# Moving sums, weight loads and a PSUM bank inside a fused attention and SiLU kernel

## The chip, the cores and the metric

The kernel runs on one core of one Trainium2 chip. The metric is the device time in microseconds (us). Three runs of the kernel before took 1318.69, 1319.69 and 1317.53 us, with a median of 1318.69.

## What is computed

The reference takes q, k and v of shape (8, 12, 448, 64), that is 8 batches of 12 heads with 448 positions. It divides each row of q and k by its root mean square and multiplies by a gain, forms softmax(q k^T / 8) v in each head, lays the heads side by side as x with 3584 rows and 768 columns, and computes a feed-forward block on it:

```
q_n, k_n = rmsnorm(q, g_q), rmsnorm(k, g_k)
attn = softmax(q_n @ k_n.T / sqrt(64))
x = (attn @ v).transpose(0, 2, 1, 3).reshape(3584, 768)
h = x @ w_in                       # 768 x 2048
out = (h * sigmoid(h)) @ w_out     # 2048 x 768
```

All inputs and the output are float32 numbers for the reference; w_in and w_out reach the chip as 64-bit words and are rounded to float32 by the kernel itself.

## The kernel before, in words

**Couples.** The attention works on 24 couples of head pairs (four heads each), three couples to a batch. In the code a couple is `c`, GROUP is 6 (the couples of two batches) and LATE is 12. For each couple, `visit(c)` issues the scores (L721), the exponentials on ScalarE (L726), and the weighted sums of v (`weigh`, L758) of this couple and the end of the last one. Then `between(c)` turns the next couple's q and k (`transpose_q` L638, `transpose_k` L656, both products with an identity on TensorE), sums the exponentials with products against ones (`sum_up`, L794), inverts the sums (L803, two halves), spreads the inverses over the partitions by DMA (`spread`, L810 and L812), and divides x by them (`divide`, L819).

**Seven products instead of eight.** The feed-forward block is computed in groups of two batches by a Strassen-type scheme (`Seven`): seven products of half-size blocks, whose operands are sums and differences. `sum_x` makes those of x: for each of three column blocks four VectorE operations of 128x448 (`right_sums`, L880, through `plus` and `minus`, L868 and L865). `sum_w_in` makes those of w_in, four steps of 128x768 for each of four chunks. A product takes six matmuls of 128x448 (L918). The products are evicted by ScalarE copies (L926, L936), VectorE sums (`plus`, L868) and GpSimd sums (L938, L939). Results of the first layer go through SiLU (L1056) and are stored to DRAM by `save` (L951).

**PSUM.** The pool ps_mm has two banks for products ("mm"). The pool ps has two tiles of two banks named "sc" (scores, transposes and, from couple 5 on, the sums of `sum_up`) and one bank each for "av0" and "av1". `bank(n)` hands out a product bank. In `sum_up` couples 0 to 4 take a product bank and couple 5 takes an "sc" tile.

**Order.** The order on every engine is that of the program text (the schedule is manual). `fill` deals the work of the products out between the couples: at every between-phase it advances a generator by a share of steps (one step is 448 columns, two matmuls), and deals a list of other pieces evenly over these steps, so that piece k of n falls after step total x k / n; a second list, `prompt`, gets one piece every three steps. From couple 6 to 11 the share is 13 steps a half. Products 1 and 2 of the first two blocks of the first group are made ahead, from couple 3 on (`make_ahead`), and kept in DRAM.

**Rounding of w_in.** `Rounder` brings 24 pieces of w_in (128x512 words of 64 bits, 0.5 MB each) in by SyncE DMAs (`load`, L85), splits them on ScalarE (`open`, L100 and L101), and rounds them on VectorE (L123, L126, L130) and GpSimd (L134) in `round`. Every `round` tries two more loads, each of which is issued when its buffer is free. The strings in `halves` and `visits` (L1388, L1389) say in which half of which couple pieces are opened ("o") and rounded ("r"). The sums of w_in are placed by `sums_halves` and `sums_visits`; those of the last chunk stand in couple 10:

```
sums_halves[8] = [(3, step) for step in range(4)]
```

**The first group's sums.** In `visit(6)`, after `divide(5)`, twelve VectorE operations make the sums of x for the first group, first steps 0 and 1 of the three column blocks, then steps 2 and 3. In `between(5)` the order is: sums of the exponentials, `divide(4)`, the two reciprocals and their DMAs, then the transposes for couple 6.

**The opening.** Before couple 0, TensorE runs unused products of the identity with itself (`keep_busy`, L407), six and then four. `transpose_q(0)` then turns q in two halves, each of which waits for VectorE's scaling of its rows (L511).

Of the kernel before, what the change touches and what calls it, by code (L numbers as in the profile page):

```python
# [11 lines left out]
F32 = mybir.dt.float32  # L12
# [15 lines left out]
BANK = 512  # L28
# [36 lines left out]
class Rounder:  # L65
# [3 lines left out]
    def __init__(self, nc, pieces):  # L69
        self.nc = nc  # L70
        self.pieces = pieces
        self.loaded = self.opened = self.rounded = 0

    def load(self):

# [29 lines left out]
    def round(self):  # L105

        i = self.rounded
        if i == len(self.pieces):
            return
        while self.opened <= i:
            self.open()
        self.rounded += 1
        dst, src, (_, raw), low = self.pieces[i]
        if src.dtype == I64:
            nc = self.nc  # L120
            wi = dst.bitcast(I32)
            high = raw.rearrange("p (n two) -> p n two", two=2)[:, :, 1]
            nc.vector.tensor_scalar(  # L123
                out=dst, in0=dst, scalar1=HIGH_MIN, scalar2=HIGH_MAX, op0=ALU.max, op1=ALU.min
            )
            nc.vector.tensor_scalar(  # L126
                out=wi, in0=wi, scalar1=3, scalar2=0x3FFFFFF8,
                op0=ALU.logical_shift_left, op1=ALU.bitwise_and,
            )
            nc.vector.scalar_tensor_tensor(  # L130
                out=wi, in0=high, scalar=-(1 << 30), in1=wi,
                op0=ALU.bitwise_and, op1=ALU.bitwise_or,
            )
            nc.gpsimd.tensor_tensor(out=wi, in0=wi, in1=low, op=ALU.add)  # L134
        for _ in range(2):
            self.load()


class Room:
# [6 lines left out]
    def __init__(self, nc, pool, w_in, z):  # L146
        P = z.P
        self.NC = z.NF // self.CHUNK
        self.size1 = z.NW * self.COLS
        self.size2 = 3 * z.NW // 2 * self.COLS // 2  # L150
        self.all = pool.tile([P, self.NC * (self.size1 + self.size2)], F32, name="W")
        self.rest = self.all[:, ds(self.NC * self.size1, self.NC * self.size2)]


        n = 2 * self.COLS
        bits = self.rest.bitcast(I32)
        pieces, before = [], {}
        for i in range(self.NC):
            for c in range(z.NW):
                number = len(pieces)  # L160
                raw = (number, number, 6 + number % 3, 7 + number % 2)[i]
                if 9 <= number < 12:
                    raw -= 6
                words = bits[:, ds(raw * n, n)]
                pieces.append(
                    (
                        self.chunk(i)[:, ts(c, self.COLS)],
                        w_in[ts(c, P), ts(i, self.COLS)],
                        (
                            before.get(raw),  # L170
                            words,
                        ),
                        words.rearrange("p (n two) -> p n two", two=2)[:, :, 0],
                    )
                )
                before[raw] = number
        self.w_in = Rounder(nc, pieces)

    def chunk(self, i):
        return self.all[:, ds(i * self.size1, self.size1)]  # L180
# [355 lines left out]
def bounded(  # L536
# [4 lines left out]
    HW, HF = z.NW // 2, z.NF // 2  # L541
# [87 lines left out]
    def transpose_q(c):  # L629

        t = ps.tile([P, 2, BANK], F32, name="sc", bufs=2)
        both = [t[:, i] for i in range(2)]
        if c == 0:
            both[1] = ps.tile([P, BANK], F32, name="av1")
        for i in range(2):
            for j in range(J):
                rows = q_of(c)[0:R, ts(i * J + j, 2 * D)]
                nc.tensor.transpose(both[i][:, ts(j, R)], rows, ident[0:R, 0:R])  # L638
            if c == 0:
                (nc.scalar.copy, nc.vector.tensor_copy)[i](qT[:, i], both[i][:, 0:S])  # L640
        if c > 0:
            nc.scalar.copy(qT, t[:, :, 0:S])
        if GROUP - 2 <= c <= GROUP:
            load_q(c + 2)
        elif c > GROUP + 1:
            load_q(c + 1)
# [129 lines left out]
    def sum_up(c):  # L776

        n = D // 2
        early = c < GROUP
        t = bank(S) if c < GROUP - 1 else ps.tile([P, 2, BANK], F32, name="sc", bufs=2)[:, 0, 0:S]
        terms = [(0, lambda: weights(c, 0))]
        if early:
            terms = [(0, lambda: weights(c, LEFT - 1))] + terms + [(1, None)]
        if c == GROUP - 1:
            terms.insert(1, (0, lambda: weights(c, 1)))
        for k, (which, w) in enumerate(terms):
            if k == len(terms) - 2:  # L790
                yield
            for h in range(2):
                for i in range(2):
                    nc.tensor.matmul(  # L794
                        t[ds(h * D + i * n, n), :],
                        ones[:, which + i if which else 0],
                        left_weights(c)[:, h] if which else w()[:, i, h],
                        start=(k == 0), stop=(k == len(terms) - 1),
                    )

        def invert(half):
            rows = ts(half, S // 2)
            nc.vector.reciprocal(out=factors(c)[0][:, rows], in_=t[:, rows])  # L803

        def spread():
            mine = [a.rearrange("(h i p) s -> i h p s", h=2, i=2) for a in factors(c)]
            queues = (nc.sync, nc.gpsimd if c == GROUP - 1 else nc.sync)
            for h in range(2):
                for i in range(2):
                    queues[h].dma_start(mine[1][i, h], mine[0][1, h])  # L810
            for h in range(2):
                queues[h].dma_start(mine[0][1, h], mine[0][0, h])  # L812

        yield [lambda: invert(0), lambda: (invert(1), spread())]
# [575 lines left out]
    for c in range(GROUP // 2):  # L1390
        halves[2 * (c - GROUP)], halves[2 * (c - GROUP) + 1] = "rr", "o"
    sums_halves = {-6: [(0, 0)], -4: [(0, 1)], -3: [(0, 2)], -2: [(0, 3)]}
    sums_halves[8] = [(3, step) for step in range(4)]
    sums_visits = {GROUP + 1: 1, GROUP + 3: 2}

    def weights_in(c, half):
# [14 lines left out]
    def visit(c):  # L1411
# [17 lines left out]
        if c > 0:  # L1429
            weigh(c - 1, LEFT - 1, 1)  # L1430
            if c - 1 < EARLY:
                for i in range(2):
                    nc.vector.tensor_copy(x_of(c - 1, i), sums[i])
                run_all(beside[1:2])
                if c == GROUP // 2 + 1:
                    divide(c - 2, None)
                if inverting:
                    while len(inverting) > 1:
                        inverting.pop(0)()
                    if c > 1:  # L1440
                        divide(c - 2, None)
            else:
                divide(c - 1, sums)
                if c == GROUP:
                    for steps in (range(2), range(2, 4)):
                        for i in range(HW):
                            sum_x(last_two(c), i, steps)
                run_all(beside[1:2])
                if GROUP < c < NC and c % GROUP == 0:
                    for i in range(1, HW):  # L1450
                        sum_x(last_two(c), i)
                weights_in_visit(c)
            if c + 1 < NC:
                loads["vrest"](c + 1)
# [28 lines left out]
    def run_all(work):  # L1483
        for piece in work:
            piece()

    def between(c):

        def transposes_and_sums():
            summing = sum_up(c)  # L1490
            if c < GROUP:
                next(summing)
            if c == GROUP - 1:
                reciprocals = next(summing)
                divide(c - 1, None)
                run_all(reciprocals)
                return
            if c < LATE - 1:
                transpose_k(c + 1)
            reciprocals = next(summing)  # L1500
            if LATE - 1 <= c < NC - 1:
                reciprocals += [lambda: flip(c + 1, "k"), gain]
            if GROUP // 2 < c < EARLY:
                divide(c - 1, None)
            return reciprocals
# [25 lines left out]
        if c >= LATE - 2:  # L1531
            if c == LATE - 2:
                prompt.append(pair_up)
            queries = prompt[3:] + [lambda: sum_squares(c + 2)]
            fill(weights_in(c, 1), prompt[:3] + [lambda: run_all(queries)])
        else:
            fill(weights_in(c, 1) + (further[:2] if c >= GROUP else []), prompt)
        if c % GROUP == GROUP - 1:
# [15 lines left out]
    load_q(2)  # L1554
    for _ in range(2):
        room.w_in.load()
    transpose_k(0)
    transpose_q(0)
    for c in range(NC):
# [230 lines left out]
```

## Time and profile before

| what | value |
|---|---|
| median of three runs | 1318.69 us |
| the profiled execution, device time | 1321.97 us |
| its span | 1320.2 us |
| TensorE matmuls busy (PE) | 1298.7 us, 98% |
| VectorE busy (DVE) | 951.1 us, 72% |
| ScalarE busy (ACT) | 505.4 us, 38% |
| GpSimd busy (POOL) | 362.6 us, 27% |
| mean granted TensorE clock | 0.995 |
| HBM traffic | 93.98 MB read, 41.29 MB written |

The profile is one execution on the chip. PE is TensorE's matmuls, PEld its weight loads, SP the engine that issues most DMAs. "L918" is line 918 of the kernel. In a timeline line the first number is the start in us, the second the duration, "x12" how many instructions are merged in the line, and the square brackets give the idle time of the engine before it and what ended that. The attention and the first layer take about the first 735 us of the span; after that TensorE runs the rest of the first layer and the second layer with hardly a pause.

### The profile page before, as it was taken

The page shows a single profiled execution, that of the slowest core. Times are in us where ns is not written, and L with a number is a line of the kernel's source. Part 1 is how long each engine was busy: PE and PEld are TensorE (multiplying, and loading weights), DVE is VectorE, ACT ScalarE, POOL GpSimd, SP SyncE. Part 2 cuts the span into 40 slices and gives each one's busy share as a digit, 9 for nine tenths or more (in the row PEclk, how much of TensorE's full clock was granted, in tenths as well). Part 3 has the DMA queues.
Part 4 walks back from the last instruction along what each step waited for, and adds up shares of the span by engine and source line. Part 5 has one row for each costly group of instructions (what it writes and reads, how often), then busy time and mean ns, then how long its engine had stood idle before and what let it go on. Part 6 is the DMA issues. An engine that isn't in the chain of part 4 may idle for free.

```text
span 1320.2 us, 19851 instructions
## 1 busy us (share of the span) xinstructions
PE 1298.7 (98%) x7201; PEld 833.0 (63%) x7201; DVE 951.1 (72%) x1627; ACT 505.4 (38%) x886; POOL 362.6 (27%) x230
## 2 busy tenths in 40 slices
PE   8999899999999999999999999999999999999998
PEld 4444444444444444444444455558999999999997
DVE  6998776785855555855554686698978787878785
ACT  7866555654555555454544244410000000000000
POOL 5765533353334333333420244410000000000000
PEclk9999899999999999999999999999999999999999
DMA  9675336333444444444321367412323233231411
GB/s 235 158 193 137 91 91 195 89 90 86 97 103 108 99 93 118 98 93 117 84 65 66 110 202 257 142 61 76 101 77 106 79 101 97 81 121 57 133 43 39
DMA packets 249439, 144.94 MB, mean 110 GB/s; under 512 B 184292, under 2 KB 233220, under 8 KB 249332
## 3 DMA queue, kind: packets, MB, share of 16 engines
q1 hardware_dynamic: 248672, 142.42, 38.7%
q8 instruction: 59, 0.97, 0.3%
q0 software_dynamic: 352, 0.96, 0.2%
q14 instruction: 48, 0.39, 0.1%
q10 hardware_dynamic: 308, 0.20, 0.1%
HBM read 93.98 MB, written 41.29 MB: 102 GB/s over the span
## 4 chain that ended last, share of the span: by engine, by line
PE 90%; DVE 3%; ACT 3%; issue 1%; DMA 1%; POOL 1%; SPq 0%; ACTq 0%; DVEq 0%; POOLq 0%
PE alone L1225 23%; PE mm L918 20%; PE sc L918 9%; PE av L758 9%; PE sc L721 8%; PE mm L1225 8%; PE alone L918 7%; PE alone L1262 2%; PE sc L794 1%; PE mm L794 1%; PE mm L1262 1%; ACT work L726 1%; DMA hidden<-stage 1%; PE sc L656 1%; DVE sums_x L865 1%
## 5 line engine op out<-in xcount | busy, mean ns | idle before, releaser
L726 ACT ACTIVATE work<-sc,rms 128x448 f32<-128x448 f32 x318 | 181.4, 634 | 66.2 <-PE sc L721 51.2
L918 PE MATMUL mm<-x,W 128*128 128x448 f32 x414 | 172.3, 552 | 6.3 <-DVE parts L868 4.1
L721 PE MATMUL sc<-work 64*64 64x448 f32 x1344 | 166.1, 548 | 1.7 <-ACT work L726 1.4
L772 DVE TENSOR_TENSOR work<-work 128x896 f32<-128x896 f32 (+1 forms) x114 | 124.5, 1125 | 51.4 <-PE av L758 50.9
L918 PE MATMUL mm<-sums_x,W 128*128 128x448 f32 x372 | 152.4, 543 | 1.9 <-DVE parts L868 1.9
L758 PE MATMUL av<-work,rows 64*64 64x448 f32 x1272 | 151.5, 540 | 0.7 <-DVE av L734 0.3
L496 POOL TENSOR_TENSOR rms<-rms,minus_half 128x14 f32<-128x14 f32 (+4 forms) x43 | 105.5, 2456 | 153.5 <-DVE rms L492 144.2
L918 PEld LDWEIGHTS mm<-x,W 128*128 128x128 f32 x414 | 77.8, 193 | 90.7 <-issue 75.6
L523 POOL DMA_DIRECT2D out_dram<-x x2 | 1.2, 592 | 443.3 <-DVE x L868 443.3
L918 PEld LDWEIGHTS mm<-sums_x,W 128*128 128x128 f32 x372 | 69.3, 190 | 74.8 <-issue 68.2
L1225 PE MATMUL alone<-W,rows 128*128 128x192 f32 x610 | 113.0, 326 | 0.0
L758 PEld LDWEIGHTS av<-work,rows 64*64 64x64 f32 x1272 | 57.0, 132 | 70.8 <-issue 33.9
L1225 PEld LDWEIGHTS alone<-W,rows 128*128 128x128 f32 x610 | 101.5, 190 | 0.0
L721 PEld LDWEIGHTS sc<-work 64*64 64x64 f32 x1344 | 53.5, 133 | 74.8 <-ACT work L726 30.9
L938 POOL TENSOR_TENSOR parts<-parts,stage 128x448 f32<-128x448 f32 x31 | 42.0, 1356 | 147.5 <-DVE parts L868 147.1
L918 PE MATMUL sc<-x,W 128*128 128x448 f32 x198 | 80.6, 543 | 0.0
L697 POOL TENSOR_TENSOR rms<-rms,minus_half 128x28 f32<-128x28 f32 x12 | 57.5, 4794 | 61.5 <-DVE rms L694 54.9
L1225 PE MATMUL alone<-W,work 128*128 128x192 f32 x382 | 72.2, 326 | 0.0
L1056 ACT ACTIVATE stage<-stage 128x896 f32<-128x896 f32 x63 | 57.4, 945 | 22.0 <-DVE stage L868 21.3
L803 DVE RECIPROCAL work<-sc 128x224 f32<-128x224 f32 x38 | 58.6, 1547 | 8.8 <-PE sc L794 8.6
L1235 ACT COPY rows<-alone 128x192 f32<-128x192 f32 x33 | 10.5, 318 | 141.5 <-PE alone L1225 78.1
L1225 PEld LDWEIGHTS alone<-W,work 128*128 128x128 f32 x382 | 63.8, 190 | 0.0
(258 smaller groups left out, 2262.8 us busy)
## 6 DMA issues: line engine op xcount, KB each, us to landing
hidden<-stage SPq DMA_DIRECT2D x63, 448.0 KB, 3.4
work<-hidden SPq DMA_DIRECT2D x21, 1024.0 KB, 5.2
rows<-in_moe_w_out_dram SPq DMA_DIRECT2D x32, 384.0 KB, 3.4
W<-in_moe_w_in_dram SPq DMA_DIRECT2D x22, 512.0 KB, 5.1
x<-hidden SPq DMA_DIRECT2D x7, 1024.0 KB, 5.6
work<-work SPq DMA_DIRECT2D x111, 56.0 KB, 2.0
rows<-in_q_dram SPq DMA_DIRECT2D x96, 56.0 KB, 2.2
rows<-in_k_dram SPq DMA_DIRECT2D x96, 56.0 KB, 2.2
```

Source lines behind the costliest of these rows:

```text
L496: nc.gpsimd.tensor_tensor(out=t, in0=t, in1=half, op=ALU.pow)
L697: nc.gpsimd.tensor_tensor(out=f, in0=f, in1=minus_half.to_broadcast([P, n]), op=ALU.pow)
L721: nc.tensor.matmul(two[ds(half * D, D), h, 0:S], keys[rows, ts(half, D)], qT[rows, pair, :], start=True, stop=True,)
L726: nc.scalar.activation(left_weights(c)[:, h] if j == LEFT else weights(c, j)[:, i, h], two[:, h, 0:S], AF.Exp, scale=norm.column(c, i, h, j),)
L758: nc.tensor.matmul(sums[i][ds(h * D, D), :], v, w, start=(j == 0 and step == 1), stop=(j == LEFT - 1 and step == 1),)
L772: nc.vector.tensor_tensor(out=total, in0=total, in1=more, op=ALU.add)
L803: nc.vector.reciprocal(out=factors(c)[0][:, rows], in_=t[:, rows])
L918: nc.tensor.matmul(t, self.left(name, s), self.right(name, s), start=s == ends[0], stop=s == ends[1])
L938: nc.gpsimd.tensor_tensor(out=u2, in0=u2, in1=p5, op=ALU.add)
L1056: nc.scalar.activation(t, t, AF.Silu)
L1225: nc.tensor.matmul(t, x[:, i], y, start=i == ORDER[0], stop=i == ORDER[-1])
L1262: nc.tensor.matmul(o, a[:, 2 * i + m, t], right_one(name, i)[:, m], start=n == 0, stop=n == len(steps) - 1,)
```

## The change

It has five parts. Four unused products are added in `transpose_q(0)`, two ahead of each half, into the bank "av0". The sums of couple 5 go into a product bank. The four operations of the first column block of `sum_x` for the first group move from `visit(6)` to `between(5)`, between `divide(4)` and the reciprocals. From piece 17 on, `Rounder` issues a load only if fewer than two pieces (three from piece 20 on) are loaded ahead of the rounding. The fourth step of the last chunk's w_in sums moves to the second half of couple 10, where the list of pieces is doubled with empty ones, so that it is dealt at the middle of the half.

```diff
@@ Rounder.__init__
         self.loaded = self.opened = self.rounded = 0
+        self.tight = len(pieces)
@@ Rounder.round
         for _ in range(2):
-            self.load()
+            if i < self.tight or self.loaded - self.rounded < 2 + (i > self.tight + 2):
+                self.load()
@@ Room.__init__
         self.w_in = Rounder(nc, pieces)
+        self.w_in.tight = 3 * z.NW - 1
@@ transpose_q
         for i in range(2):
+            if c == 0:
+                keep_busy(2)
             for j in range(J):
@@ sum_up
-        t = bank(S) if c < GROUP - 1 else ps.tile([P, 2, BANK], F32, name="sc", bufs=2)[:, 0, 0:S]
+        t = bank(S) if c < GROUP else ps.tile([P, 2, BANK], F32, name="sc", bufs=2)[:, 0, 0:S]
@@ the plan of bounded
-    sums_halves[8] = [(3, step) for step in range(4)]
+    sums_halves[8] = [(3, step) for step in range(3)]
+    sums_halves[9] = [(3, 3)]
@@ visit
                 if c == GROUP:
                     for steps in (range(2), range(2, 4)):
-                        for i in range(HW):
+                        for i in range(1, HW):
                             sum_x(last_two(c), i, steps)
@@ between
             if c == GROUP - 1:
                 reciprocals = next(summing)
                 divide(c - 1, None)
+                sum_x([0, 1], 0)
                 run_all(reciprocals)
                 return
@@ between
-            fill(weights_in(c, 1), prompt[:3] + [lambda: run_all(queries)])
+            steps = weights_in(c, 1)
+            fill(steps + [lambda: None] * len(steps), prompt[:3] + [lambda: run_all(queries)])
@@ end of bounded
+    idle = ps.tile([P, BANK], F32, name="av0")[:, 0:P]
+
+    def keep_busy(n):
+        for _ in range(n):
+            nc.tensor.matmul(idle, ident, ident, start=True, stop=True)
+
     transpose_k(0)
     transpose_q(0)
```

## The prediction

> **What bounds the kernel now.** I first read the page's busy rows. TensorE (PE) works 98% of the span, so only three things can shorten the program: less PE work, a hole in PE, or a faster PE clock. The change removes no product, so I went to the list of PE's waits, for the first 330 us, where the changed lines are:
>
> ```profile
> PE 1298.7 (98%) x7201; PEld 833.0 (63%) x7201; DVE 951.1 (72%) x1627; ACT 505.4 (38%) x886; POOL 362.6 (27%) x230
> PE mm L918 <- DVE parts L868: 6.0, 3, 3.4
> PE mm L918 <- DVE stage L868: 1.6, 2, 0.9
> PE av L638 <- DVE rows L511: 1.0, 1, 1.0
> PE sc L656 <- ACT work L642: 1.0, 1, 1.0
> ```
>
> The columns are total wait, times, longest. All holes come to some 12 us, under 1% of the span: that is the ceiling. Then I cut the stretches of these holes out by windows (PE busy, PEld, DVE, ACT, POOL, granted PE clock, DMA share, GB/s):
>
> ```profile
> 9.90:13.30 3.40, 3.40 (x20) 1.08 (x19) 2.54 (x5) 0.86 (x2) 2.24 (x3) 0.50 1.09 206
> 129.20:137.30 8.10, 4.70 (x15) 2.12 (x13) 8.07 (x14) 2.52 (x5) 3.36 (x1) 0.93 0.24 84
> 137.30:144.70 7.40, 7.40 (x12) 3.58 (x13) 5.76 (x8) 2.05 (x4) 2.58 (x3) 0.61 0.04 7
> ```
>
> Twice PE is busy at half clock: right after the opening, and after the hole at 133.87. In that hole DVE is full (8.07 of 8.10). The timeline says with what:
>
> ```profile
> 110.79 2.97 DVE L803 RECIPROCAL work<-sc 128x224 f32<-128x224 f32 x2 [2.44 <-PE sc L794]
> 119.16 2.02 DVE L130 SCALAR_TENSOR_TENSOR W<-W 128x512 int32<-128x512 int32 x1
> 121.64 1.14 DVE L819 TENSOR_TENSOR x<-av,work 128x448 f32<-128x448 f32 x2
> 124.05 2.37 POOL L511 TENSOR_TENSOR x<-x,rms 112x512 f32<-112x512 f32 x2
> 124.55 2.35 DVE L865 TENSOR_TENSOR sums_x<-x,sums_x 128x448 f32<-128x448 f32 x1
> 126.82 1.71 DVE L865 TENSOR_TENSOR sums_x<-x 128x448 f32<-128x448 f32 x1
> 136.60 0.61 DVE L868 TENSOR_TENSOR parts<-mm,stage 128x448 f32<-128x448 f32 x1
> 137.26 7.62 PE L918 MATMUL mm<-x,W 128*128 128x448 f32 x12 [3.40 <-DVE parts L868]
> ```
>
> The reader is to see that DVE idles 2.44 us at 108.35 and is 3.4 us late at 137.26: work is to be moved from the one place to the other. Last, the holes at 218 and 281:
>
> ```profile
> 203.88 0.43 SPq L85 DMA_DIRECT2D x<-in_moe_w_in_dram  x1
> 208.92 1.72 SPq L951 DMA_DIRECT2D hidden<-stage  x2
> 214.84 0.53 ACT L936 COPY stage<-mm 128x448 f32<-128x448 f32 x1 [5.14 <-DMA hidden<-stage]
> 219.97 2.52 PE L918 MATMUL mm<-sums_x,W 128*128 128x448 f32 x6 [1.93 <-DVE parts L868]
> 279.53 1.77 DVE L868 TENSOR_TENSOR W<-W 128x768 f32<-128x768 f32 x1
> 281.89 2.52 PE L918 MATMUL mm<-x,W 128*128 128x448 f32 x6 [0.86 <-DVE stage L868]
> ```
>
> [...] half clock from 9.92 to 13.33 and from 136.2 to 143.04, one and two windows of 3.41. [...] the window 6.50 to 9.92 holds transposes alone, and the clock fell after it. [...] the sum at 124.55 took 2.35 beside L511, against 0.62 for its like. [...] The store at 208.92 landed at 214.74, behind all that was issued since 200; a quiet one (177.31) took 2.50.
>
> **The change, part by part.** The sum is made against the profiled execution: 1321.97 us, its span 1320.2. The median of the runs, 1318.69, is 3.28 less; I subtract from that.
>
> *Four unused products in the opening.* Eight PE instructions. The L407 ones stand 213 ns apart at half clock, 107 at full: 0.85 us in two pairs. The first pair falls into PE's idle 0.49 us before 8.10, the second into its 1.01 before 9.72, so they cost nothing; at half clock the first pair would overrun by up to 0.4. They put 0.85 us of true products (25%) into the window 6.50 to 9.92. If that keeps the clock, the first scores end at 11.35 instead of 12.44 and ACT's exponentials, which PE waits for at 14.96, come 1.1 earlier. Does it suffice? The window 132.79 to 136.2, 32% busy, lost the clock; 218.13 to 221.54, 46% busy, kept it; 25% plus transposes lies about there. Bounds +0.4 (half clock) and -1.1; I take **-0.5**.
>
> *Couple 5's sums in a product bank.* PE holds product 1 of block 1 unfinished in one bank, so the sums get the other. The K transposes no longer wait for ACT L642: 111.64 instead of 112.63, and ACT L658, L926, L100, L101, L467 follow 1.0 earlier. DVE L468 (116.85, idle 0.76 before) can take 0.76 of it. Then L130 runs from about 118.4, ahead of POOL's L134 (119.33, held up by POOL's own DMA issues), and takes 0.69, not 2.02. Price: product 2 now needs the bank of the sums, so it waits for the second reciprocal (113.76) from 113.2: 0.55 of the 1.0, or as much for L926 if it gets the other bank. No gain on PE by itself; divide 5 is what counts. It can't start before POOL's spread DMA has landed (120.63): 120.7 instead of 121.64, **0.94**.
>
> *First sums behind divide 4.* Four of twelve L865/L868-type sums (0.54 apart where free) move to 108.35 in DVE's queue. Behind them stand the reciprocals, whose DMAs divide 5 awaits. 4 x 0.54 = 2.16 fits the 2.44 idle; POOL then runs L496, beside which the sums at 122.7 took 0.62. So they cost nothing; without that cover, up to 4 x 2.35, 7 us more. They issue no DMA. Behind divide 5 (now ending at 121.77) eight sums are left: five before POOL's L511 at 124.05, the sixth to 126.95, the seventh after L134 to 128.75, the eighth 129.3, against 132.40: 3.1 earlier. The same 4.2 us (two L468, L492, three L772) follow, so L868 ends at 134.1. PE arrives at 133.4 and waits 0.7 instead of 3.40; the clock holds. Then products 7 and 3, 4.5 us, to 138.6; product 4 needs L868 again, which DVE reaches after three L772 and the rounding (4.8) at 138.9: 139.55. Before: 144.72. That is 5.2 in this execution. Without a fallen clock, product 4 would have begun before at 142.8, so the clock is worth 1.9 here; the phase of the windows differs by run, and I count 1.3 (an estimate). **-4.5**; bounds -6.2 (POOL never in the way, no hole) and -2.2 (only the four sums).
>
> *w_in loads.* Following the rounding: load 20 (203.88) moves to after round 18, load 21 to after round 19, loads 22 and 23 to couple 9's end, behind the q loads at 239.7 on SP. Load 20 is 0.5 MB; at the 257 to 263 GB/s of 204 to 212 it is 2.0 us of backlog ahead of the store; at the 360 of 212 to 216, 1.5. L936 and all behind it on ACT (L467, so DVE's L468 and L868) come that much earlier; the hole of 1.93 shrinks to some 0.2: **-1.7**, bounds -1.95 and -0.9. The moved loads: 22 and 23 issue at about 240.4, are used after 258; SP then has nothing until the k loads at 249.46. Cost nothing; without that gap, ACT would wait in couple 9's end.
>
> *Couple 10's fourth sum a half later.* Nine instead of ten pieces are dealt over 13 steps, so the first W sum falls after step 8 instead of 7: behind the L868 of the product that ends at step 7, not ahead of it. The 0.86 goes. The fourth sum (0.95) lands in DVE's idle 2.64 before 295.54. The doubled list only deals it at half-way. **-0.85**, bounds -0.9 and -0.3.
>
> Sum: 0.5 + 4.5 + 1.7 + 0.85 = 7.55, so **1311.1**. After 300 us PE has next to no holes, so nothing gives it back; next in line are the new 0.95 hole at 138.6 and the old 0.62 at 183.07.
>
> **Rivals.** (a) Divide 5 does not come earlier (another landing, POOL's order), only the four sums leave: 0.5 + 2.2 + 1.7 + 0.85, **1313.4**. For it: divide 5 hangs on one DMA landing. (b) The store is late all the same, since loads 18 and 19 and the v and q loads stay ahead: 1311.1 + 1.7, **1312.8**. (c) The change doesn't do what it says: DVE, 72% busy, comes late at the next product instead and only the hole at 281 closes, 0.85: **1317.8**. (d) Slower: the extra product tile shifts which of two banks later products get. A product that gets its predecessor's bank waits for that one's eviction: 0.71 at 93.86 and 0.62 at 183.07. The page counts 414 + 372 matmuls in these banks, 131 products; if one in seven falls so, 19 x 0.66 = 12.5: **1323.6**. It decides from 12 such products on; two in 131 speak against it. (e) All at the good bound, 10: **1308.5**.
>
> **How the numbers follow.** Forecast 0.54, (a) 0.18, (b) 0.09, (c) 0.08, (d) 0.04, (e) 0.07. About 0.2% (2.6 us) is what a measurement of this kernel can tell from no change. Faster: 0.88; same: (c), 0.08; slower: 0.04. Low end: bounds 1.1 + 6.2 + 1.95 + 0.9 give 1308.5, less the 1.2 by which runs fall under the median: 1307.3. High end: 0 + 2.2 + 0.9 + 0.3 give 1315.3, plus 0.7 of spread: 1316.0. Outside lie (c), (d) and some tails.
>
> **What would show it.** DVE's four sums stand before the reciprocals, which still start within 0.2 us of the last L794; the hole before product 7 is under 1.5 us and no window after it has half clock; ACT L936 waits under 3.5 us for the store near 212; no hole at couple 10's third product. PE clock 1.00 near 10 us would settle the opening. I am wrong if the reciprocals come late, if PE waits more than 1.5 us for the bank of couple 5's sums, or if many products wait for their predecessor's eviction.

## The result, and the profile after

| | median | lowest to highest |
|---|---|---|
| before, six runs | 1319.01 us | 1317.53 to 1320.65 |
| after, six runs | 1311.65 us | 1311.32 to 1311.92 |
| ratio, with its 95% interval | 0.9943 | 0.9931 to 0.9956 |

The change makes the kernel 7.4 us faster; the forecast was 1311.1. The profiled execution of after took 1311.68 us with a span of 1309.9, so 10.3 us less than the profiled one of before (1321.97, span 1320.2). The difference to the 7.4 of the medians is at least in part the clock: the profiled execution of before has three windows of 3.41 us at half clock, and a mean granted clock of 0.995. Of the other first six executions of before the clock is not on record; later ones lie between 1317.9 us (at 0.999) and 1322.8 us (at 0.996). Those of after lie at 0.999 and 1.000, with one at 0.998.

The page's busy row, of after:

```profile
PE 1294.2 (99%) x7209; PEld 832.3 (64%) x7209; DVE 950.1 (73%) x1627; ACT 505.0 (39%) x886; POOL 360.8 (28%) x230
```

PE has eight instructions more (the unused products) and yet 4.5 us less busy time: a busy microsecond at half clock does half the work (products of 448 columns start 747 ns apart between 136.21 and 143.03 of before, and 376 ns apart behind that, at full clock). The other 5.8 us of the span are time in which PE no longer stands idle. PE's waits in the first 330 us, of after (total, times, longest):

```profile
PE mm L923 <- DVE parts L873: 2.4, 3, 1.1
...
PE mm L923 <- ACT stage L931: 0.8, 1, 0.8
PE mm L923 <- DVE stage L873: 0.7, 1, 0.7
```

L868 of before is L873 here, and L926 is L931 (the lines moved by one to five). The 6.0 of before became 2.4, the 1.6 became 0.7. The 1.0 for L642 is gone, and a wait of 0.8 for L931 is new. The windows, of after, with the same columns as before:

```profile
9.90:13.30 3.40, 2.89 (x28) 0.83 (x27) 2.77 (x6) 1.92 (x4) 2.50 (x3) 1.00 0.82 143
127.00:132.50 5.50, 4.37 (x13) 1.92 (x11) 5.46 (x10) 2.51 (x5) 3.35 (x1) 1.00 0.33 118
132.50:139.00 6.50, 5.98 (x18) 2.98 (x19) 5.69 (x8) 2.06 (x4) 1.66 (x2) 1.00 0.00 0
```

The clock is 1.00 in all three. The timeline around the first group's sums, of after:

```profile
106.49 0.61 DVE L870 TENSOR_TENSOR sums_x<-x 128x448 f32<-128x448 f32 x1
...
108.93 2.97 DVE L808 RECIPROCAL work<-mm 128x224 f32<-128x224 f32 x2
...
112.10 2.52 PE L923 MATMUL mm<-x,W 128*128 128x448 f32 x6 [0.81 <-ACT stage L931]
...
116.45 2.22 DVE L131 SCALAR_TENSOR_TENSOR W<-W 128x512 int32<-128x512 int32 x1
116.81 1.30 POOL L135 TENSOR_TENSOR W<-W 128x512 int32<-128x512 int32 x1
119.13 1.14 DVE L824 TENSOR_TENSOR x<-av,work 128x448 f32<-128x448 f32 x2
121.53 2.36 POOL L514 TENSOR_TENSOR x<-x,rms 112x512 f32<-112x512 f32 x2
122.03 2.35 DVE L870 TENSOR_TENSOR sums_x<-x,sums_x 128x448 f32<-128x448 f32 x1
...
127.01 0.61 DVE L870 TENSOR_TENSOR sums_x<-x,sums_x 128x448 f32<-128x448 f32 x1
...
132.48 4.78 PE L923 MATMUL mm<-x,W 128*128 128x448 f32 x12 [1.13 <-DVE parts L873]
137.78 1.02 PE L923 MATMUL mm<-sums_x,W 128*128 128x448 f32 x2 [0.52 <-DVE parts L873]
```

The early sums stand where DVE idled for 2.44 us, and the reciprocals behind them start without a wait. The hole ahead of product 7 (the line at 132.48) is 1.13 instead of 3.40. Product 4 begins at 137.78, where it had begun at 144.72. Last, couples 8 and 10, of after:

```profile
201.93 1.10 SPq L956 DMA_DIRECT2D hidden<-stage  x2
203.09 0.73 SPq L86 DMA_DIRECT2D x<-in_moe_w_in_dram  x1
206.07 0.53 ACT L941 COPY stage<-mm 128x448 f32<-128x448 f32 x1 [3.12 <-DMA hidden<-stage]
211.19 2.52 PE L923 MATMUL mm<-sums_x,W 128*128 128x448 f32 x6
...
271.58 0.62 DVE L873 TENSOR_TENSOR stage<-mm,parts 128x448 f32<-128x448 f32 x1
272.12 1.24 DVE L873 TENSOR_TENSOR W<-W 128x768 f32<-128x768 f32 x1
272.26 2.52 PE L923 MATMUL mm<-x,W 128*128 128x448 f32 x6
```

The w_in load now follows the store, the copy waits 3.12 instead of 5.14, and the product at 211.19 has no wait. In couple 10 the sum for the product (271.58) stands ahead of the first W sum (272.12), and the product at 272.26 doesn't wait either.

Where the 10.3 us of the two profiled executions went can be read from the start of the same instruction in both. The opening gives 1.3 and the stretch to 107 us another 0.5. Couple 5's end and couple 6 give 5.1, couple 8 2.0, couple 10 0.9; the rest, about 0.5, lies behind. The 0.5 before 107 us arises near 80 us, where none of the five parts has its place; two of the runs below lose time there as well.

### The profile page after: what moved, and what is told of

Same layout as the page of the kernel before. It is cut to its first block, busy times and chain, and to the rows that moved or that the text cites. A ratio compares the mean times of both kernels' runs of the same rounds, so it can differ in the third digit from the quotient of the medians.

```text
span 1309.9 us, 19866 instructions
## 1 busy us (share of the span) xinstructions
PE 1294.2 (99%) x7209; PEld 832.3 (64%) x7209; DVE 950.1 (73%) x1627; ACT 505.0 (39%) x886; POOL 360.8 (28%) x230
## 4 chain that ended last, share of the span: by engine, by line
PE 94%; DVE 2%; ACT 2%; issue 1%; POOL 0%; ACTq 0%; DVEq 0%; POOLq 0%
PE alone L1230 23%; PE mm L923 22%; PE av L763 9%; PE sc L726 9%; PE sc L923 9%; PE mm L1230 8%; PE alone L923 7%; PE alone L1267 2%; PE sc L799 1%; PE mm L799 1%; PE mm L1267 1%; PE sc L643 1%; PE sc L661 1%; ACT work L731 1%; DVE work L777 0%
## 5 line engine op out<-in xcount | busy, mean ns | idle before, releaser
L777 DVE TENSOR_TENSOR work<-work 128x896 f32<-128x896 f32 (+1 forms) x114 | 124.6, 1125 | 50.0 <-PE av L763 49.5
L923 PEld LDWEIGHTS sc<-x,W 128*128 128x128 f32 x198 | 36.9, 190 | 39.6 <-issue 37.2
```

The source lines that it names most:

```text
L777: nc.vector.tensor_tensor(out=total, in0=total, in1=more, op=ALU.add)
L923: nc.tensor.matmul(t, self.left(name, s), self.right(name, s), start=s == ends[0], stop=s == ends[1])
```

## The experiments

All edits are against the kernel after. The kernel after itself was run again beside them on two chips, and took 1311.88 us (1311.36 to 1312.45, ratio 0.9937, 0.9925 to 0.9949) and 1311.83 us (1311.48 to 1312.45, ratio 0.9929, 0.9916 to 0.9943). With the first runs that makes three medians from 1311.65 to 1311.88, some 1311.8. The kernel before took 1320.00 and 1321.20 there. A further chip ran the first kernels without the products, the bank, the sums and the loads; the kernel before took 1320.38 on it and the kernel after wasn't run there, so these four are held against the 1311.8 of the others. The executions of the kernel after spread over about 1 us on one chip, so differences of a few tenths of a microsecond are not read. What was expected of the two repeats:

> The changed kernel unaltered, so that the others of this chip have it beside them. Both theories: 1311.7 to 1313.0, 7 to 8 us under the kernel before on the same chip; full clock through the opening and at couple 6.

> The changed kernel unaltered, beside the others of this call. 1311.4 to 1312.5.

**Each part taken out by itself.** Without the unused products:

```diff
-            if c == 0:
-                keep_busy(2)
```

> The changed kernel without the four unused products of the opening. Theory (the products keep the clock through the window that else holds only transposes): in executions where the clock falls, couple 0's first exponentials start 1.1 us later and the time is 1.3 us longer; median 1312.6, between 1312.0 and 1313.0, and the runs spread more than the 0.6 us of the changed kernel. Rival (the phase of the windows was lucky in the profile after, the products do nothing): 1311.65 within 0.3.

Measured: 1313.72 us (1312.14 to 1315.58), ratio 0.9947 (0.9934 to 0.9961). Run again beside the kernel after on one chip:

> The changed kernel without the unused products, a second time, to be held against the unaltered one on the same chip. Theory (the clock falls in the opening in most executions): median 0.8 to 1.5 us over the unaltered kernel, and a wider spread. Rival (the 2 us of its first measurement came from couple 8's store): within 0.4 of it, the same spread.

Measured: 1313.86 (1313.43 to 1315.71), 2.0 us more than the kernel after. The window that ends near 9.4 us and the one behind it (columns as before), in the profile of the first run:

```profile
6.00:9.41 3.41, 1.91 (x14) 1.23 (x13) 2.85 (x8) 2.61 (x4) 3.41 (x3) 1.00 1.10 281
9.40:12.80 3.40, 3.09 (x16) 1.42 (x20) 2.16 (x4) 0.22 (x1) 2.42 (x2) 0.50 1.11 173
```

and of the second run:

```profile
5.95:9.36 3.41, 1.94 (x14) 1.25 (x13) 2.84 (x8) 2.66 (x4) 3.41 (x3) 1.00 1.06 269
9.40:12.80 3.40, 2.57 (x24) 1.01 (x28) 2.57 (x6) 1.41 (x3) 2.50 (x3) 1.00 0.98 170
```

The same program, with windows that begin 0.05 us apart and are 56 and 57% busy, lost the clock in one execution and kept it in the other. With the products (or with transposes in their place, below) nine profiles show that it was kept: in eight of them couple 0's second stretch of scores begins at 12.59 to 12.62, against 13.79 in the first run here, and the ninth has windows at 1.00. In the first run PE stays 1.0 to 1.4 us behind the kernel after from here to couple 7: that is what the clock of the opening costs in this execution.

Both expectations of this cost (a median of 1312.6, and 0.8 to 1.5 us) were too low, because the products are worth more than the clock. In both profiles without them the store of couple 8 landed later, and a hole opened there of 1.71 and 2.02, against none, 0.47 and 0.20 in the three of the kernel after. Of the second run, ScalarE's copy that waits for the store, and PE's waits of the first 330 us:

```profile
210.13 0.53 ACT L939 COPY stage<-mm 128x448 f32<-128x448 f32 x1 [5.27 <-PE sc L797]
PE mm L921 <- DVE parts L871: 4.4, 4, 2.0
```

The copy waits 4.92 in the first run and 5.27 here, and 3.12 and 3.40 in two profiles of the kernel after. This second profile is the slowest of its five executions, 1315.71, and it lost no clock window before the end: its 4.1 us over the kernel after on the same chip (1311.59) come from couple 8 (1.8), from holes of 0.85 at 61.38 and 0.64 at 80.12 and the time around them (1.9), and from a hole at couple 6 that is 0.36 longer. A like hole near 80 us stands in one other profile (0.91 at 79.52, with the loads as before). The same DMAs are issued in the same order, though the store is issued 0.6 to 0.8 us sooner behind the loads; why it lands later I could not find in the traces. It stays open, and so does the share of the 2.0 that is the clock's.

Couple 5's sums back in an "sc" tile:

```diff
-        t = bank(S) if c < GROUP else ps.tile([P, 2, BANK], F32, name="sc", bufs=2)[:, 0, 0:S]
+        t = bank(S) if c < GROUP - 1 else ps.tile([P, 2, BANK], F32, name="sc", bufs=2)[:, 0, 0:S]
```

> The changed kernel with couple 5's sums back in a score tile. Theory (the bank buys ScalarE 1.0 us and costs TensorE 0.8 for product 1's copy, so that divide 5 comes some 0.5 us earlier): 1312.2, with a hole of 1.0 before couple 6's K transposes and none before product 2. Rival (the wait for ScalarE's copy eats the gain): 1311.65 within 0.3. Second rival (the bank, not the moved sums, closed the hole at couple 6): 1314 or more.

Measured: 1312.74 (1312.08 to 1314.58), ratio 0.9945 (0.9931 to 0.9958), some 0.9 above 1311.8, with ranges that overlap. Its profile has the hole ahead of the K transposes again, and none for L931:

```profile
110.75 0.98 PE L661 MATMUL sc<-ident,rows 128*128 128x128 f32 x7 [1.00 <-ACT work L647]
```

Product 7 begins at 132.93, where the three profiles of the kernel after have 132.04 to 132.48. So PE itself gains 1.00 and pays 0.81 with the bank, and 0.45 to 0.89 in all; that the rest comes from divide 5 (119.43 here, 118.67 to 119.13 there) fits, but wasn't tested alone.

All twelve sums behind divide 5 again:

```diff
-                        for i in range(1, HW):
+                        for i in range(HW):
...
-                sum_x([0, 1], 0)
```

> The changed kernel with all twelve operations of the first group's sums behind divide 5, as before. Theory (four sums at 0.54 plus the clock that falls after the longer hole): the hole before product 7 grows from 1.13 to about 3.3 us, and half clock follows in most executions; 1315.3, between 1314.0 and 1316.5. Rival (VectorE catches up before product 4, the hole costs nothing in the end): 1312 or less.

Measured: 1315.03 (1314.43 to 1315.69), ratio 0.9960 (0.9947 to 0.9974), 3.2 above 1311.8. The hole ahead of product 7 is 3.26, and the window behind it has half clock:

```profile
131.06:134.47 3.41, 0.15 (x2) 0.01 (x1) 3.41 (x5) 2.50 (x5) 3.23 (x1) 1.00 0.00 0
134.50:137.90 3.40, 3.40 (x5) 1.76 (x6) 3.34 (x4) 1.50 (x3) 0.00 (x0) 0.50 0.00 0
```

Three of the five executions have a mean clock of 0.997 and two 0.998. One window is worth 0.0013 of the mean; 0.998 also occurs without one (the profile at 1315.71 above, which has half clock only in its last 4.1 us), so the window is known to fall in the profiled execution, and is likely in all.

The loads as before:

```diff
-        self.w_in.tight = 3 * z.NW - 1
```

> The changed kernel with w_in loads issued as early as their buffers allow. Theory (load 20 stands ahead of the store in the DMA queue): the store of couple 8 lands about 1.9 us later after its issue and a hole of 1.9 us opens on TensorE; 1313.6, between 1313.2 and 1314.0. Rival (the store is quick because everything else moved): 1311.65 within 0.3.

Measured: 1314.00 (1312.91 to 1316.80), ratio 0.9951 (0.9937 to 0.9964), 2.2 above 1311.8. The hole of couple 8 is back, and in this execution a window at half clock follows it:

```profile
214.47 3.94 PE L922 MATMUL mm<-sums_x,W 128*128 128x448 f32 x6 [1.98 <-DVE parts L872]
212.02:215.43 3.41, 1.43 (x5) 0.59 (x4) 3.38 (x5) 2.17 (x4) 2.87 (x2) 1.00 0.65 139
215.40:218.80 3.40, 3.40 (x6) 1.50 (x5) 2.95 (x6) 0.00 (x0) 1.92 (x2) 0.50 0.20 51
```

This execution is the slowest of its five (1316.80); 1.6 us of it were lost near 80 us, where the loads' change has no place.

The fourth W sum back in couple 10's first half:

```diff
-    sums_halves[8] = [(3, step) for step in range(3)]
-    sums_halves[9] = [(3, 3)]
+    sums_halves[8] = [(3, step) for step in range(4)]
```

> The changed kernel with all four sums of the last w_in chunk in couple 10's first half. Theory (the first of them is dealt ahead of an eviction that TensorE waits for): a hole of 0.86 at couple 10's third product, 0.85 us longer than the changed kernel unaltered. Rival (the hole came from VectorE and GpSimd contending and moves by chance): the same as the changed kernel within 0.3.

Measured: 1312.47 (1311.93 to 1313.44), 0.6 above the kernel after on the same chip, with ranges that overlap. The hole in couple 10 is back:

```profile
272.53 2.52 PE L923 MATMUL mm<-x,W 128*128 128x448 f32 x6 [0.90 <-DVE stage L873]
```

What the five cost when taken out, 2.0, 0.9, 3.2, 2.2 and 0.6, makes 8.9; the gains in the three comparisons were 7.4, 8.1 and 9.4. The sum fits, but it doesn't show that the parts are independent: taking out the products brings back couple 8's hole, which is also what the loads' part closes, so that stage is counted twice in the 8.9. What is shown is that each of the other four brings back its own hole when it is taken out.

**Products or transposes in the opening.** My forecast put the lost clock of the opening down to the transposes, which stand alone in the window of 6.50 to 9.92; that one window was all it had to show. The rival is that the window was just not busy enough (1.85 of 3.41 us). First, transposes in place of the products:

```diff
-                keep_busy(2)
+                turn_idle(4)
...
+    def turn_idle(n):
+        for _ in range(n):
+            nc.tensor.transpose(idle, ident, ident)
```

> The changed kernel with eight unused transposes of the identity in the place of the four unused products (one instruction of 128 columns for each of theirs). Theory (transposes don't keep the clock): half clock after the opening in most executions, about 1 us longer than the changed kernel and runs spread over 2 us or more, as without the products. Rival (any TensorE work keeps it): full clock at 10 us and the time of the changed kernel within 0.3.

Measured: 1311.89 (1311.34 to 1312.56), as the kernel after (1311.88), and the clock is 1.00 in the opening (from 4.49 to 11.31). Then 64 transposes ahead of the first half, which fill two whole windows:

```diff
-                keep_busy(2)
+                turn_idle(64 * (1 - i))
```

> The changed kernel with 64 unused transposes of the identity, 6.9 us at full clock, ahead of couple 0's first half, in the place of the four products: two windows long, so that at least one whole window holds nothing but transposes, whatever its phase. Theory (transposes count for little): half clock is granted during them, they take 9 us or more, and the time is 8 to 12 us longer. Rival (they count as any work; what counts is the busy share): full clock, 6.9 us, and a time 6 to 7 us longer.

Measured in one run: 1318.06, 6.2 us longer than the kernel after (the 64 take 7.15 us). The second of the two windows with nothing but transposes, and the one behind it, in its profile:

```profile
11.25:14.65 3.40, 3.40 (x33) 3.40 (x32) 0.00 (x0) 0.00 (x0) 0.64 (x1) 1.00 0.99 232
14.65:18.10 3.45, 2.69 (x26) 1.26 (x24) 2.31 (x5) 1.65 (x4) 0.09 (x1) 1.00 0.83 215
```

The clock stayed at 1.00. For these float32 transposes the rival is right: in both runs they kept the clock. That a transpose counts for somewhat less than a product isn't excluded by these two runs.

**What holds product 4.** Two empty pieces were put ahead of couple 6's first list, so that its additions for the sums of the exponentials (`late`, L777) and the rounding behind them are dealt two places later, to see whether only their place made PE wait:

```diff
+        late = [lambda: None] * (2 * (c == GROUP)) + late
         fill(late + weights_in(c, 0) + (further[2:] if c >= GROUP else further[:2]))
```

> The changed kernel with two empty pieces ahead of couple 6's first list, so that the first of its four additions is dealt behind the eviction of product 6, and the rounding behind that of product 7. Theory (VectorE's order, not its total work, makes the two holes left at couple 6): the holes of 1.13 and 0.52 go, 1.6 us shorter than the changed kernel. Rival (VectorE is short of time in couple 6, the holes come back at products 3 and 4): the same as the changed kernel within 0.3.

Measured: 1312.54 (1311.56 to 1314.31), no gain on the same chip. The holes of 1.13 and 0.52 are gone, and 0.23 and 0.94 stand at 142.63 and 145.39 instead. VectorE is busy for 18.1 of the 18.3 us from 126.7 to 145.0 in this profile: it is short of time there, and this other order only moves the hole.

**The DMAs that GpSimd issues.** POOL waits 2.8 to 3.2 us for its own spread DMA in couple 5 in the three profiles of the kernel after, and 3.5 us in the kernel before, until it can round and scale. If all six go to SyncE:

```diff
-        queues = (nc.sync, nc.gpsimd if c == GROUP - 1 else nc.sync)
+        queues = (nc.sync, nc.sync)
```

> The changed kernel with all six spreading DMAs of couple 5 on SyncE, none on GpSimd. Theory (GpSimd's rounding step of couple 5 meets VectorE's L131 only because GpSimd waits for its own DMAs first): L131 before divide 5 takes 0.7 us instead of 2.2, divide 5 comes 0.5 to 1.0 us earlier after the last ones product than in the changed kernel, the hole before product 7 shrinks by as much; 0.5 us shorter than the unaltered kernel. Rival (the landing on SyncE alone is later and becomes the bound of divide 5): 0.5 us longer.

Measured: 1310.49 (1310.43 to 1310.90), ratio 0.9919 (0.9905 to 0.9932), 1.3 us under the kernel after on the same chip; its five executions all lie under the five of that kernel (1311.48 to 1312.45). Its profile:

```profile
119.32 2.04 POOL L514 TENSOR_TENSOR x<-x,rms 112x512 f32<-112x512 f32 x2
119.42 1.16 DVE L824 TENSOR_TENSOR x<-av,work 128x448 f32<-128x448 f32 x2 [1.21 <-DMA work<-work]
120.50 1.35 DVE L870 TENSOR_TENSOR sums_x<-x 128x448 f32<-128x448 f32 x1
...
121.88 1.60 DVE L870 TENSOR_TENSOR sums_x<-x,sums_x 128x448 f32<-128x448 f32 x1
...
126.20 0.62 DVE L870 TENSOR_TENSOR sums_x<-x,sums_x 128x448 f32<-128x448 f32 x1
...
131.69 2.52 PE L923 MATMUL mm<-x,W 128*128 128x448 f32 x6
```

The gain came, but not by the way of the theory. L131 takes 0.69, but it does so in the kernel after on this chip as well. Divide 5 is later, not earlier (119.42; 118.67 there), and waits for the spread DMA, as the rival had it. What is earlier is POOL: L514 runs from 119.32 (121.39 there), mostly beside the divide, which takes its usual 1.16. Two sums are stretched, to 1.35 and 1.60, in place of 2.35 and 1.71, so the sums end at 126.82 instead of 127.17, and the hole ahead of product 7 (0.78 there) is gone. Of the 1.3 us of the medians the two profiled executions show 0.7.

## Why the prediction was right, step by step

*The sum.* For the profiled execution it gives 0.5 + 5.2 + 1.7 + 0.85 = 8.25, and 10.3 came; for the medians 7.55, and 7.4, 8.1 and 9.4 came. On equal clock the gain is steadier: two runs of before at 0.999 took 1317.92 and 1318.02, and the four of after at 0.999 on that chip 1311.36 to 1312.03, so 6.3. How often before lost its clock is at least part of the rest. That 7.4 lies so near 7.55 is in part luck: in the profiles the opening gave 0.8 more than its term and the loads 0.3 more, and 1.0 came at places that no term names.

*The opening: direction right, size and reason wrong.* "I take -0.5" was too little: -1.32 in the two profiles, and 2.0 on the medians, part of it a store at couple 8 that the working didn't connect with the opening. The term was taken between two bounds because I could not say whether the window would suffice, and the good bound (-1.1) was still short. (The high end of the range takes 0 for this term, where the bad bound is +0.4.) The products cost nothing in their idle places, as predicted: in the profile of the second run without them, where the clock held, couple 1's K transposes begin at 21.72, as in a profile with them on the same chip. Within a pair the instructions start 111 to 125 ns apart in the profile of after, where I had taken 107, half of 213. The reason given, that the window of 6.50 to 9.92 holds transposes alone, fell with the two runs on transposes. It had looked sound because that window is 54% busy and lost the clock, where one of products at 46% kept it; but that this share settles the clock of the next window was my estimate, and busy time misleads here, as the last section shows.

*The bank: price right, payer wrong, one sub-step half right.* I let product 2 wait for the second reciprocal; it waited 0.81 for ACT's copy of product 1 (L931), the alternative I had named, because it got that product's bank. "L130 takes 0.69, not 2.02" (L131 now) failed in the profile of after, with 2.22: I had kept POOL's L134 where it was, at 119.33, but POOL came earlier along with DVE, to 116.81, since its wait for its own DMA shrank as well. Of the two other profiles of the kernel after, one repeats this (2.17), and in the other, with nothing altered:

```profile
116.49 0.69 DVE L131 SCALAR_TENSOR_TENSOR W<-W 128x512 int32<-128x512 int32 x1
...
117.13 1.31 POOL L135 TENSOR_TENSOR W<-W 128x512 int32<-128x512 int32 x1
118.67 1.16 DVE L824 TENSOR_TENSOR x<-av,work 128x448 f32<-128x448 f32 x2 [0.95 <-PE av L763]
```

POOL starts 0.3 us later, DVE is through in 0.69, and the hole ahead of product 7 is 0.78 instead of 1.13. So the step can come true and is decided by some tenths of a microsecond. Divide 5 there waits for the products of `weigh` on PE, not for the DMA that I had named as its limit. It came 0.65 earlier (beyond the 1.86 that all of PE was ahead by) in the first profile; 0.94 was predicted.

*The early sums: right.* They lie in DVE's idle time, and the reciprocals start 0.07 after the last product that they need (within 0.2 was predicted). The twelve sums end 2.9 earlier beyond the lead; 3.1 was predicted, though not by the same way: POOL's L514 came forward as well, so three sums, not five, ran ahead of it. The fourth met it (2.35) and the fifth met L135 (1.71), in place of the sixth and the seventh. The hole ahead of product 7 is 1.13, in one of three profiles 0.78 (0.7 predicted), and that ahead of product 4 0.52 (0.95 predicted). Product 4 begins 5.1 earlier beyond the lead; 5.2 was predicted for this execution. The clock held. Taking out this part cost 3.2, clock included.

*The loads: right, a little too small.* 2.0 in the profiles and 2.2 on the medians, where 1.7 was taken and 1.95 was the bound. The copy waits 2.0 us less for the store, as the working said of 0.5 MB in front of it.

*Couple 10: right.* 0.86 in the profiles, with 0.85 predicted; 0.6 on the medians.

*The rivals.* (a), a divide 5 that stays, is refuted by its 0.65. (b), a late store, is refuted in the kernel after; it is what happens without the unused products, for a reason that is open. (c) fell with the hole at couple 6 cut to 1.13 and that at couple 8 closed. (d), products that get their predecessor's bank: PE's waits of the first 330 us show one such product more (0.81), besides those of before. (e) would have needed no hole ahead of product 7, and there is one.

## What to carry to other kernels

In a kernel whose bound engine is 98% busy, each of its larger holes could be followed to one late instruction. Taking out one part doesn't only measure that part's own stage: without four unused products in the opening, a store 200 us later landed late in both profiles. An instruction that is made earlier can bring its neighbours on other engines along (POOL's rounding came 2.52 us sooner, at 116.81, where PE was ahead by 1.86): don't hold a second engine at its old time when you work out whether two of them will meet. And a hole can cost more than its own length: the one of 3.26 without the early sums and the one of 1.98 with the loads as before were each followed by 3.4 us at half clock, while one of 1.93 in the kernel before was not. The same program has a spread of times: the kernel before took 1317.92 us in one execution (at 0.999) and 1322.78 in another (at 0.996). Before a change of a few microseconds is called understood, compare executions window by window: the mean clock alone doesn't tell a lost window from a longer stretch of half clock at the very end.

## What the runs showed of the hardware

- In the profile of before the granted clock changed at 9.91, 13.33, 136.21 and 143.03 us: 3.41, 122.88 (36 times 3.413) and 6.83 apart. A window here is a step of 3.41, counted from these changes. The clock's record begins at 6.50 there and at 5.64 in the profile of after, so the windows lie differently in the two.
- Transposes of float32 kept the TensorE clock: 64 of them in a row, two windows of nothing else (7.85 to 14.65), at 1.00, with 1.00 behind them (above).
- PE's busy time in a window doesn't order what followed. From full clock, half clock came after 1.43 us (couple 8, with the loads as before), 1.85 (before, opening) and 1.91 (no unused products), and full clock stayed after 1.57 (before, couple 8), 1.70 (no unused products, couple 8) and 1.94 (no unused products, second run). Of before, a window that lost it and one that kept it:

```profile
6.50:9.91 3.41, 1.85 (x14) 1.17 (x13) 2.82 (x6) 1.98 (x3) 3.41 (x3) 1.00 1.14 275
218.13:221.54 3.41, 1.57 (x4) 0.87 (x5) 3.24 (x3) 1.55 (x3) 3.41 (x2) 1.00 0.31 60
```

  Busy time draws an instruction of 128 columns 0.27 to 0.33 us long, though the next of its kind starts 0.109 us later (0.096 for 112 columns, 0.376 for 448). Counted with that spacing, each from its start, these two windows come to some 1.18 and 1.47 us (an estimate), in the order of what followed. The first holds transposes and the second products, and no run shows how busy a window has to be.
- At half clock, a window with PE busy for 2.35 of 3.41 us (before, 136.21 to 139.62) was followed by half clock again. Full clock came behind 3.41 (before, 139.62 to 143.03), 3.42 (before, 9.91 to 13.33) and 3.40 (no early sums, 134.50 to 137.90).
- DVE beside POOL: L131 took 2.22 us with L135 starting 0.36 after it, 2.17 with 0.30 and, in the kernel before, 2.02 with 0.17; it took 0.69 with L135 starting 0.45 (transposes in place of the products) or 0.64 after. POOL's part hardly differed (1.30, 1.31, 1.30, 1.39 and 1.31). So where they met it was DVE that took longer, although it had started first each time; the runs don't show why.
